# Gated recurrence and gated state-space block on one core: the opening in chunks, weights loaded later, two turns in another order

## The chip, the cores and the metric

The kernel runs on one core of one Trainium2 chip. The metric is the time of one execution on the device in microseconds (us). A core has a matrix engine (PE, TensorE) with its own weight load (PEld), a vector engine (DVE), a scalar engine (ACT), a GpSimd engine (POOL) and a sync engine (SP) that here only issues transfers (DMAs). Each engine works through its own list of instructions in order; semaphores tie the lists together. SBUF is the on-chip memory of 128 partitions, PSUM the eight banks into which PE writes.

## The reference, cut to what matters

A gated linear recurrence over 4 batches, 8 heads, 768 steps and a head width of 48, whose output, heads side by side, is the input of a gated state-space block:

```
for t in range(768):                       # q, k, v, alpha: (4, 8, 768, 48)
    state = alpha[t][:, None] * state + outer(k[t], v[t])
    y[t] = q[t] @ state
x = heads side by side                     # (4, 768, 384)
val, gate = split(x @ w_in)                # w_in (384, 1024)
h[t] = exp(A_log[0]) * h[t-1] + val[t]     # a scan, per channel
out = (silu(gate) * h) @ w_out             # w_out (512, 384)
```

All inputs are float32 but w_in and w_out, which arrive as 64-bit floats and are made into float32 on the chip.

## The kernel before, in words

The 4 x 768 steps are cut into 12 groups of 256 steps. Group m goes through the recurrence as follows (lines of the kernel before).

- Its alpha, q and k are loaded (L410 for whole tiles, L421 for the first groups) with steps on partitions and are turned so that the head width lies on partitions: for groups 0 to 3 by PE against an identity (`turned`, L680, either by matmuls, L694, or by transposes, L689 and L690) with copies out of PSUM by ACT (L702) or DVE (L701); from group 4 on by DVE itself (`turn`, L595).
- Two scans on DVE give the running products P of alpha from the front (`scan_P`, L630) and V from the back (`scan_V`, L649). k times V gives Zk (L614), q times P gives Zq (L605).
- `scores` (PE, L744) multiplies Zk with Zq in blocks of 64 steps, `masks` cuts them to the lower triangle: on DVE (L754, L759), ACT (L756, L760, L764) and, from group 3 on, POOL (L762).
- `values` (PE, L778; for group 0 L862) gives the part of y from the own block, `states` (PE, L810) each block's contribution to the state, which POOL (`add_up`, L828, L830) or DVE (`add_banks`, L838; group 0: L879) adds up; `carried` (PE, L791; group 0: L870) applies the states to q.
- `join` copies y out of PSUM (ACT, L904, L905) and moves the pieces of heads to their places in xT by DMA (L907), issued by SP and POOL; group 0 needs no moves (`first_join`, L884).

Then the second block: `project(n, cc)` (PE, L927) multiplies group n's xT by one of four 128-column units of w_in, val first, then gate, into two PSUM banks; DVE scans val (L932), ACT takes silu of the gate (L940), DVE or POOL multiplies them (L942). `output(n)` (PE, L956) multiplies by w_out, ACT copies the result (L950), SP stores it.

The weights' 64-bit words are loaded in units (`load_w`, L453; `load_w_out`, L459) and converted in three parts: `low` on ACT (L544), two operations on DVE (L553, L555), an integer add on POOL (L557). Before, unit 2 of the loads holds the third and fourth 128 columns together.

The order is written by hand: what the Python code calls first stands first in every engine's list. The loop over n (turn n) projects group n while group n + 1 or n + 2 goes through the recurrence. In a steady turn: `second(n+1)` (values, states, sums), four projections with steps of DVE's work for a later group between them (`go(count)` runs that many of the seven steps of `products`: turn a, scan P, turn k, scan V, Zk, turn q, Zq), `third(n+1)` (carried, values, join), `first(n+2)` (scores, masks), and `output(n)`. Four PSUM banks named mm are shared in rotation by turns, projections, outputs and the second half of the scores.

Of the kernel before, what the change touches and what calls it, by code (L numbers as in the profile page):

```python
# [346 lines left out]
def fast(  # L347
# [22 lines left out]
    nc = tc.nc  # L370
# [18 lines left out]
    p2 = pool("p2", 2)  # L389
    ps_at = pool("ps_at", 1, space=PS)  # L390
# [56 lines left out]
    units = [range(0, 1), range(1, 2), range(2, 4)]  # L447
# [45 lines left out]
    def constants():  # L493
# [45 lines left out]
    def low(i):  # L539
        bits, w = bits_of(i)  # L540
        r = p2.tile([C, UW], I32, tag="wr", name="wr")
        lows[i] = r.rearrange("p (a n) -> p a n", a=w.shape[1])
        halves = lows[i].bitcast(U16).rearrange("p a (n two) -> p a n two", two=2)
        nc.scalar.activation(halves[:, :, :, 0], bits[:, :, :, 0], AF.Copy, scale=2.0 ** -29)  # L544

    def convert(i):
        if i not in lows:
            low(i)
        bits, w = bits_of(i)
        r = lows.pop(i)  # L550
        halves = r.bitcast(U16).rearrange("p a (n two) -> p a n two", two=2)
        quarters = bits.rearrange("p a n two -> p a (n two)").bitcast(U16).rearrange("p a (n four) -> p a n four", four=4)
        nc.vector.tensor_scalar(out=w.bitcast(U32), in0=bits[:, :, :, 1], scalar1=3, scalar2=0x3FFFFFFF,  # L553
                                op0=ALU.logical_shift_left, op1=ALU.bitwise_and)
        nc.vector.tensor_scalar(out=halves[:, :, :, 1], in0=quarters[:, :, :, 3], scalar1=0xC000, scalar2=None,  # L555
                                op0=ALU.bitwise_and)
        nc.gpsimd.tensor_tensor(out=w.bitcast(I32), in0=w.bitcast(I32), in1=r, op=ALU.add)  # L557
# [126 lines left out]
    def turned(m, name, js, t):  # L684
        raw = steps_of(name, m)
        tp = t[:, 0:len(js) * C].rearrange("p (j x) -> p j x", j=len(js))
        if (m, name) in ((1, "k"), (1, "q"), (3, "a")):
            for n, j in enumerate(js):
                nc.tensor.transpose(tp[:, n], raw[:, ds(ROW + j * D - 64, C)], ident)  # L689
                nc.tensor.transpose(tp[0:64, n], raw[:, ds(j * D, 64)], ident)  # L690
            return tp.rearrange("p j (c h) -> p h c j", h=4)
        for n, j in enumerate(js):
            for i in range(2):
                nc.tensor.matmul(tp[ds(64 * i, 64), n], raw[:, ds(i * ROW + j * D, 64)], ident,  # L694
                                 start=True, stop=True, skip_group_check=True)
        return tp.rearrange("p j (c h) -> p h c j", h=4)

    def copy_turned(to, js, tp, engine=None):
        place = by_runs(to)[:, :, :, js.start:js.stop]
        if engine:  # L700
            return engine.tensor_copy(out=place, in_=tp)  # L701
        return nc.scalar.activation(place, tp, AF.Copy)  # L702

    def turn_over(m, name, to, tags=(None, None)):
        size = NJ // len(tags)
        copies = []
        for n, tag in enumerate(tags):
            js = range(size * n, size * (n + 1))
            copy = copy_turned(to, js, turned(m, name, js, bank(tag)), nc.vector if n % 2 and tag else None)
            if tag:  # L710
                for other in copies[(n + 1) % 2::2]:
# [3 lines left out]
    def alphas(m, tags=(None, None)):  # L715
        turn_over(m, "a", by_place(als[m % 2])[:, :, 1:GP], tags)
# [31 lines left out]
    def masks(m):  # L748
        sc = [[t[:, 0:4 * (L + D)].rearrange("p (h x) -> p h x", h=4) for t in pair] for pair in scs.pop(m)]
        mb = mask[:, None, :]  # L750
        if m < NG:
            for c in range(G):
# [162 lines left out]
    def project(n, cc, late=False):  # L915
# [10 lines left out]
        for vg, kk in order:  # L926
            nc.tensor.matmul((pv, pg)[vg], w_ins[cc][:, kk, vg, :], xT[:, kk, :],  # L927
                             start=(kk == 0), stop=(kk == NK - 1))
# [10 lines left out]
        sg = p2.tile([C, GC], FP32, tag="sg", name="sg")  # L939
# [43 lines left out]
    alphas(0, ("s0", "s1", "y1", "y0"))  # L983
    tq = straighten(0, "q")
    tk = straighten(0, "k")
    alphas(1)
    P = scan_P(0)
    V = scan_V(0, P, False)
    halves = [range(0, NJ // 2), range(NJ // 2, NJ)]
    parts = [turned(1, "k", js, bank()) for js in halves]  # L990
# [3 lines left out]
    scores(0)  # L994
    tk = plain("k")
    for js, part in zip(halves, parts):
        copy_turned(tk, js, part)
    low(0)
    parts = [turned(1, "q", js, bank()) for js in halves]
    convert(0)  # L1000
    nc.gpsimd.memset(raws["a"][0:1, 0:1], 0.0)
    load_steps("a", 2, [nc.sync])
    load_w(units[2], nc.sync)
    masks(0)
    low(1)
    first_values(True)
    st = states(0)
    convert(1)
    first_states(st)
    tq = plain("q")  # L1010
    for js, part in zip(halves, parts):
        copy_turned(tq, js, part)
    last = P[:, :, GC]
    nc.scalar.activation(ratio[:, 0], last, AF.Copy, scale=1.0 / FIRST_PRODUCT)
    nc.scalar.activation(lower[:, :, 0], last, AF.Copy)
    for name in "kqa":
        load_steps(name, 2 + (name == "a"), [nc.sync])
    load_v(1, nc.sync)
# [31 lines left out]

    for n in range(N):
        m = n + 1
        if n == 0:
            V = scan_V(1, P)
            f0 = project(n, 0)
# [3 lines left out]
            f1 = project(n, 1)  # L1059
            convert(2)  # L1060
            alphas(2)
            low(3)
            first(m)
            f0()
            f1()
            tk = straighten(2, "k")
            load_raw("k", 3, nc.sync)
            P = scan_P(2)
            tq = straighten(2, "q")
            V = scan_V(2, P)  # L1070
            convert(3)
            junk(1)
            low(4)
            f2 = project(n, 2)
            values(m, True)
            st = states(m)
            add_banks(m, st)
# [8 lines left out]
        elif n == 1:  # L1086
# [8 lines left out]
            add_banks(m, st)  # L1095
            f3()
# [26 lines left out]
        else:  # L1123
            if n == 2:
                first(m)
                go(1)
                f0 = project(n, 0)
                second(m)
                go(2)
            else:  # L1130
                second(m)
                go(4)
                f0 = project(n, 0)
            f0()
# [11 lines left out]
            load_raw("q", n + 3, nc.sync)  # L1146
# [4 lines left out]
            go(1)  # L1151
# [3 lines left out]
            first(m + 1)  # L1155
# [8 lines left out]
        if 0 < n < N - 1:  # L1164
            output(n)
    return value
# [61 lines left out]
```

## Time and profile before

| | us |
|---|---|
| timed runs, median (lowest to highest of 3) | 279.6 (279.18 to 279.66) |
| profiled execution | 279.43 |
| its span | 277.7 |
| PE busy | 268.8 |
| DVE busy | 218.3 |
| POOL busy | 122.4 |
| ACT busy | 108.6 |

The span runs from the first to the last instruction; the profiled execution's own time is 1.73 us longer. In a row of the timeline or of the chain of waits stand the start and the length in us, the engine, the line and what was written; in brackets is the idle time of the engine before it and what ended it. Matmuls in float32 appear in the trace as two rows each, transposes as one. PE's granted clock is 1.00 over the whole span.

### The profile page before, as it was taken

The page shows a single profiled execution, that of the slowest core. Times are in us where ns is not written, and L with a number is a line of the kernel's source. Part 1 is how long each engine was busy: PE and PEld are TensorE (multiplying, and loading weights), DVE is VectorE, ACT ScalarE, POOL GpSimd, SP SyncE. Part 2 cuts the span into 40 slices and gives each one's busy share as a digit, 9 for nine tenths or more (in the row PEclk, how much of TensorE's full clock was granted, in tenths as well). Part 3 has the DMA queues.
Part 4 walks back from the last instruction along what each step waited for, and adds up shares of the span by engine and source line. Part 5 has one row for each costly group of instructions (what it writes and reads, how often), then busy time and mean ns, then how long its engine had stood idle before and what let it go on. Part 6 is the DMA issues. An engine that isn't in the chain of part 4 may idle for free.

```text
span 277.7 us, 9598 instructions
## 1 busy us (share of the span) xinstructions
PE 268.8 (97%) x4056; PEld 217.0 (78%) x4056; DVE 218.3 (79%) x281; ACT 108.6 (39%) x244; POOL 122.4 (44%) x141
## 2 busy tenths in 40 slices
PE   7999999999989999899999999999999999999995
PEld 5988887876678688488688688688688688787874
DVE  7979998898798995995895995996995993079540
ACT  2577763461332532341542433433434425213111
POOL 8141223130068574563473584484384476435000
PEclk9999999999999999999999999999999999999999
DMA  6949993845919777487468587576687501201201
GB/s 196 295 140 309 296 262 78 205 88 139 267 48 238 149 199 182 103 214 163 103 181 199 114 205 164 130 197 155 152 186 159 144 0 27 77 1 33 71 5 59
DMA packets 51599, 41.18 MB, mean 148 GB/s; under 512 B 27360, under 2 KB 49536, under 8 KB 51552
## 3 DMA queue, kind: packets, MB, share of 16 engines
q1 hardware_dynamic: 48752, 37.50, 53.1%
q0 software_dynamic: 1408, 2.03, 2.8%
q10 hardware_dynamic: 1392, 0.99, 1.2%
q8 instruction: 33, 0.54, 0.9%
q14 instruction: 14, 0.11, 0.2%
HBM read 32.54 MB, written 4.72 MB: 134 GB/s over the span
## 4 chain that ended last, share of the span: by engine, by line
PE 92%; DVE 3%; DMA 1%; POOL 1%; issue 1%; ACT 1%; SPq 0%; DVEq 0%; ACTq 0%
PE mm L927 45%; PE mm L956 21%; PE y L791 4%; PE y L778 4%; PE mm L744 3%; PE s L744 3%; PE s L810 3%; PE mm L694 2%; PE mm L1189 2%; DMA raw_a<-in_alpha_dram 1%; POOL AK L762 1%; DVE P L630 1%; DVE V L649 1%; PE mm L689 1%; PE y L862 1%
## 5 line engine op out<-in xcount | busy, mean ns | idle before, releaser
L927 PE MATMUL mm<-xT,w_in 128*128 128x256 f32 x576 | 128.9, 382 | 0.6 <-ACT xT L884 0.6
L927 PEld LDWEIGHTS mm<-xT,w_in 128*128 128x128 f32 x576 | 108.1, 190 | 16.3 <-issue 0.8
L956 PE MATMUL mm<-w_out,f_last 128*128 128x384 f32 x160 | 54.1, 492 | 1.3 <-DVE A L759 1.3
L940 ACT ACTIVATE sg<-mm 128x256 f32<-128x256 f32 x48 | 18.4, 384 | 85.8 <-PE mm L927 80.3
L956 PEld LDWEIGHTS mm<-w_out,f_last 128*128 128x128 f32 x160 | 29.7, 190 | 21.1 <-issue 1.4
L830 POOL TENSOR_TENSOR sum<-sum,dS 128x192 f32<-128x192 f32 x30 | 33.2, 1108 | 27.3 <-PE mm L927 13.5
L942 POOL TENSOR_TENSOR f_last<-sg,hh 128x256 f32<-128x256 f32 x36 | 30.9, 862 | 30.6 <-ACT sg L940 23.1
L932 DVE TENSOR_TENSOR_SCAN hh<-a_dec,hh,mm 128x256 f32<-128x256 f32 x32 | 23.4, 732 | 15.4 <-PE mm L927 15.2
L630 DVE TENSOR_TENSOR_SCAN P<-al,lower 128x1028 f32<-128x1028 f32 x12 | 31.1, 2595 | 0.6
L649 DVE TENSOR_TENSOR_SCAN V<-al,ends 128x1028 f32<-128x1028 f32 x12 | 28.3, 2356 | 0.4
L907 POOL DMA_DIRECT2D xT<-yst x40 | 20.5, 517 | 13.1 <-ACT yst L904 11.8
L950 ACT ACTIVATE o_sb<-mm 128x384 f32<-128x384 f32 x22 | 10.8, 491 | 38.4 <-PE mm L956 38.4
L762 POOL TENSOR_TENSOR AK<-AK,mask 128x512 f32<-128x512 f32 x9 | 13.2, 1464 | 17.2 <-ACT AK L760 17.2
L759 DVE TENSOR_TENSOR A<-s,mask 128x256 f32<-128x256 f32 x9 | 3.8, 425 | 21.5 <-PE s L744 21.5
L557 POOL TENSOR_TENSOR w_in<-w_in,wr 128x768 int32<-128x768 int32 x4 | 7.3, 1826 | 26.0 <-DVE wr L555 17.0
L595 DVE STREAM_TRANSPOSE k<-raw_k 128x1024 f32<-128x1024 f32 x9 | 18.3, 2033 | 0.0
L595 DVE STREAM_TRANSPOSE q<-raw_q 128x1024 f32<-128x1024 f32 x9 | 18.2, 2022 | 0.0
L778 PEld LDWEIGHTS y<-AK,v 64*64 64x64 f32 x352 | 12.1, 134 | 6.4 <-issue 5.0
L595 DVE STREAM_TRANSPOSE al<-raw_a 128x1024 f32<-128x1024 f32 x8 | 16.3, 2041 | 0.1
L778 PE MATMUL y<-AK,v 64*64 64x64 f32 x352 | 14.5, 221 | 1.0 <-POOL AK L762 1.0
L791 PEld LDWEIGHTS y<-Zq,sum 48*64 48x64 f32 x656 | 11.8, 134 | 4.3 <-issue 4.1
L791 PE MATMUL y<-Zq,sum 48*64 48x64 f32 x656 | 14.4, 221 | 0.6 <-issue 0.6
(158 smaller groups left out, 392.2 us busy)
## 6 DMA issues: line engine op xcount, KB each, us to landing
v<-in_v_dram SPq DMA_DIRECT2D x22, 192.0 KB, 3.3
out_dram<-o_sb SPq DMA_DIRECT2D x22, 192.0 KB, 2.1
raw_k<-in_k_dram SPq DMA_DIRECT2D x18, 184.0 KB, 3.4
raw_q<-in_q_dram SPq DMA_DIRECT2D x18, 184.0 KB, 3.8
raw_k<-in_k_dram SPq DMA_DIRECT2D x18, 176.0 KB, 3.8
raw_q<-in_q_dram SPq DMA_DIRECT2D x18, 176.0 KB, 4.1
raw_a<-in_alpha_dram SPq DMA_DIRECT2D x16, 184.0 KB, 5.0
raw_a<-in_alpha_dram SPq DMA_DIRECT2D x16, 176.0 KB, 5.1
```

The source lines that it names most:

```text
L595: nc.vector.transpose(out=by_runs(to).rearrange("p h c j -> p h j c"), in_=raws[name][:, 0:4 * ROW].rearrange("p (h j d) -> p h j d", h=4, ...
L630: nc.vector.tensor_tensor_scan(out=P, data0=al[:, 0:4 * GP], data1=lower.rearrange("p h t -> p (h t)"), initial=0.0, op0=ALU.mult, op1=ALU ...
L649: nc.vector.tensor_tensor_scan(out=V[:, ::-1], data0=al[:, 1:4 * GP + 1][:, ::-1], data1=ends.rearrange("p h t -> p (h t)")[:, ::-1], init ...
L778: nc.tensor.matmul(ys[m][i][ds(64 * s, 64), e, ds(c * C + h * L, L)], v_sb[rows, c, 4 * i + p, :], As[i][rows, c, p, :], start=across and ...
L791: nc.tensor.matmul(ys[m][i][ds(64 * s, 64), e, ds(u * L, L)], Ss[j][rows, p, :], Zqs[m % 2][rows, u, p, D:], start=False, stop=True, skip_ ...
L830: nc.gpsimd.tensor_add(Ss[j][:, :, 0:D], Ss[j - 1][:, :, 0:D], part)
L907: engines[n % len(engines)].dma_start(out=xT[to, a], in_=st[rows, i, e])
L927: nc.tensor.matmul((pv, pg)[vg], w_ins[cc][:, kk, vg, :], xT[:, kk, :], start=(kk == 0), stop=(kk == NK - 1))
L932: nc.vector.tensor_tensor_scan(out=hh, data0=a_dec[:, cc:cc + 1].to_broadcast([C, GC]), data1=pv, initial=prev_h[cc][:, GC - 1:GC] if n % ...
L940: nc.scalar.activation(sg, pg, AF.Silu)
L942: f = lambda: engine.tensor_mul(fs[n][cc], sg, hh)
L956: nc.tensor.matmul(os[c], fs[n][cc][:, ds(c * C, C)], w_outs[cc // 2][:, cc % 2, :], start=(cc == 0), stop=(cc == NI - 1))
```

## The change

It has five parts.

1. **Opening by chunks.** The first group's alphas are turned by 32 matmuls of 64 x 64 (`first_alphas`) instead of 16 of 128 x 64, and those that need only the half of the heads whose DMA is issued on ACT's queue come first. The first q is turned in an order by halves (`first_q`). The first k and the second alpha are turned by transposes. Memsets on DVE go: those of the sums' pad columns become copies on ACT, those of dS and K0 fall away. Of the second k only one half is turned ahead of the first scores, the other behind them; the first half of the **second q** is turned behind the states, the other, by matmuls, behind the carried work. The masks of group 0 stand ahead of the first weights' conversion on DVE.
2. **Second weights behind the scans.** The conversion of w_in's second unit is split: `low(1)` behind `first_join`, `high(1)` behind the scans P and V of group 1, `add_low(1)` behind the first projection. The alphas of group 2 are turned between the first and the second projection. Units 2 and 3 are loaded apart, unit 3 behind k, q and alpha. The signal that lets alpha of group 2 be loaded over the old one is an ACT copy from the last state's sum instead of a POOL memset.
3. **Projection in halves.** In turn 0 the gate half of `project(0, 2)` stands behind values and states of group 1 (`between`). The products of silu and scan for the first two projections move from turn 0 to turn 1, and the silu tiles have a pool of four buffers.
4. **w_out** is loaded behind the moves of y of group 1 and no longer in the opening; k, q and alpha of group 3 are loaded behind it.
5. **Two turns reordered** (`late = (1, 3)`). In turn 2 and turn 4 `second(n+1)` stands behind the second projection instead of ahead of or behind the first. In turn 3 `first(5)` stands behind `output(3)` instead of ahead of it. In turn 4 the steps of `go` and the loads are spread anew.

```diff
-    units = [range(0, 1), range(1, 2), range(2, 4)]
+    units = [range(i, i + 1) for i in range(NI)]
...
-        for t in dS[0] + dS[1]:
-            nc.vector.memset(t[:, :, :, D:64], 0.0)
-        for t in sums:
-            nc.vector.memset(t[:, :, D:64], 0.0)
-        nc.vector.memset(K0[:, :, :, D:], 0.0)
...
+    def first_alphas():
+        raw, to = steps_of("a", 0), by_runs(by_place(als[0])[:, :, 1:GP])
...
+        def turn_quarter(j, i, r):
+            rows = ds(64 * r, 64)
+            nc.tensor.matmul(tps[j // 4][r][ds(64 * i, 64), j % 4], raw[rows, ds(i * ROW + j * D, 64)],
+                             ident[rows, rows], start=True, stop=True, skip_group_check=True)
+
+        for j in range(2):
+            for r in range(2):
+                turn_quarter(j, 1, r)
+        for j in range(NJ):
+            for r in range(2):
+                turn_quarter(j, 0, r)
+                if j + 2 < NJ:
+                    turn_quarter(j + 2, 1, 1 - r)
...
+                copy = nc.vector.tensor_copy(out=place, in_=part) if r else \
+                    nc.scalar.activation(place, part, AF.Copy)
...
-    def project(n, cc, late=False):
+    def project(n, cc, late=False, between=None):
...
+        passes(order[:NK] if between else order)
...
+        if between:
+            between()
+            passes(order[NK:])
+        sg = gates.tile([C, GC], FP32, tag="sg", name="sg")
...
-    alphas(0, ("s0", "s1", "y1", "y0"))
-    tq = straighten(0, "q")
+    first_alphas()
+    for t in sums:
+        nc.scalar.activation(t[:, :, D:64], wide_S[0][:, 0:4 * (64 - D)].rearrange("p (j d) -> p j d", j=4), AF.Copy)
+    tq = first_q()
     tk = straighten(0, "k")
     alphas(1)
     P = scan_P(0)
...
     V = scan_V(0, P, False)
...
+    part = turned(1, "k", halves[0], bank())
     for c in range(G):
         scaled_k(0, tk, V, c)
         scaled_q(0, tq, P, c)
...
+    for c in range(G):
+        scores(0, (c,))
+    part = turned(1, "k", halves[1], bank())
+    masks(0)
+    low(0)
+    high(0)
+    add_low(0)
+    copy_turned(tk, halves[1], part)
+    first_values(True)
+    st = states(0)
+    part = turned(1, "q", halves[0], bank())
+    first_states(st)
+    copy_turned(tq, halves[0], part)
+    nc.scalar.activation(raws["a"][0:1, 0:1], sums[3][0:1, 0, 0:1], AF.Copy)
     load_steps("a", 2, [nc.sync])
     load_w(units[2], nc.sync)
...
+    load_w(units[3], nc.sync)
     load_v(1, nc.sync)
     P = scan_P(1)
     first_carried((1,))
     first_values(False)
     first_carried((2, 3))
+    part = turned(1, "q", halves[1], bank(), False)
     first_join()
+    low(1)
+    copy_turned(tq, halves[1], part)
...
-    for half in range(2):
-        load_w_out(half, nc.sync)
...
         if n == 0:
             V = scan_V(1, P)
-            f0 = project(n, 0)
+            high(1)
+            fs_late = [project(n, 0)]
+            add_low(1)
+            alphas(2)
...
-            f1 = project(n, 1)
+            fs_late.append(project(n, 1))
             convert(2)
-            alphas(2)
...
+            f2 = project(n, 2, between=across_and_states)
             alphas(3)
             third(m)
-            for name in "qa":
+            for half in range(2):
+                load_w_out(half, nc.sync)
+            for name in "kqa":
                 load_raw(name, 3 + (name == "a"), nc.sync)
...
+    late = (1, 3)
...
             if n == 2:
                 first(m)
-                go(1)
-                f0 = project(n, 0)
-                second(m)
-                go(2)
-            else:
+            if n - 1 not in late:
                 second(m)
                 go(4)
-                f0 = project(n, 0)
+            else:
+                go(n // 2)
+            f0 = project(n, 0)
             f0()
-            load_raw("k", n + 3, nc.sync)
-            load_raw("a", n + 3, nc.sync)
-            go(1)
+            if n == 2:
+                go(2)
+            if n != 4:
+                load_raw("k", n + 3, nc.sync)
+                load_raw("a", n + 3, nc.sync)
+                go(1)
             f1 = project(n, 1)
             f1()
+            if n - 1 in late:
+                second(m)
+            if n == 4:
+                go(2)
+                load_raw("k", n + 3, nc.sync)
+                load_raw("a", n + 3, nc.sync)
...
-            go(1)
+            go(2 if n == 4 else 1)
+            load_raw("q", n + 3, nc.sync)
             f3 = project(n, 3)
             f3()
             third(m)
-            first(m + 1)
+            if n not in late:
+                first(m + 1)
...
         if 0 < n < N - 1:
             output(n)
+        if n > 1 and n in late:
+            first(m + 1)
```

More of the change, by code (lines that the diff above doesn't have):

```diff
@@ L548, in convert @@
             low(i)
[L549 to L557, printed above, removed]
+        high(i)
+        add_low(i)
     def check_w(i):
@@ L696, in turned @@
         return tp.rearrange("p j (c h) -> p h c j", h=4)
[L698 to L705, printed above, removed]
-        copies = []
[L707 to L711, printed above, removed]
+    halves = [range(0, NJ // 2), range(NJ // 2, NJ)]
@@ L718, in straighten, with turn_over, alphas @@
+    def turn_over(m, name, to):
+        for js in halves:
+            copy_turned(to, js, turned(m, name, js, bank()))
+    def alphas(m):
+        turn_over(m, "a", by_place(als[m % 2])[:, :, 1:GP])
     def straighten(m, name):
@@ L987, in fast @@
     P = scan_P(0)
+    last = P[:, :, GC]
+    nc.scalar.activation(ratio[:, 0], last, AF.Copy, scale=1.0 / FIRST_PRODUCT)
+    nc.scalar.activation(lower[:, :, 0], last, AF.Copy)
     V = scan_V(0, P, False)
-    halves = [range(0, NJ // 2), range(NJ // 2, NJ)]
-    parts = [turned(1, "k", js, bank()) for js in halves]
+    part = turned(1, "k", halves[0], bank())
     for c in range(G):
@@ L993, in fast @@
         scaled_q(0, tq, P, c)
[L994 to L997, printed above, removed]
[L998 to L1001 removed]
+    tk, tq = plain("k"), plain("q")
+    copy_turned(tk, halves[0], part)
+    for c in range(G):
+        scores(0, (c,))
+    part = turned(1, "k", halves[1], bank())
+    masks(0)
+    low(0)
+    high(0)
[7 more added lines that the diff above has]
+    nc.scalar.activation(raws["a"][0:1, 0:1], sums[3][0:1, 0, 0:1], AF.Copy)
     load_steps("a", 2, [nc.sync])
     load_w(units[2], nc.sync)
[L1004 to L1015, printed above, removed]
     for name in "kqa":
         load_steps(name, 2 + (name == "a"), [nc.sync])
+    load_w(units[3], nc.sync)
     load_v(1, nc.sync)
```

85 lines of the change are left out of this document (59 added, 26 removed).

## The prediction, made before the changed kernel was run

> **What bounds the kernel now.** I read the page's busy line and chain first, then what PE waited for.
>
> ```profile
> span 277.7 us, 9598 instructions
> PE 268.8 (97%) x4056; PEld 217.0 (78%) x4056; DVE 218.3 (79%) x281; ACT 108.6 (39%) x244; POOL 122.4 (44%) x141
> ...
> PE 92%; DVE 3%; DMA 1%; POOL 1%; issue 1%; ACT 1%; SPq 0%; DVEq 0%; ACTq 0%
> ```
>
> PE (the matrix engine) is busy for 97% of the span and carries 92% of the chain that ends last. The profiled execution took 279.43 us, 1.73 beside its span of 277.7; the three timed runs have a median of 279.6. The change takes next to no work off PE, so it can only gain where PE stands idle, and it loses wherever it makes PE wait anew. The waits of PE, by releaser (total, times, longest):
>
> ```profile
> PE mm L956 <- DVE A L759: 1.3, 1, 1.3
> PE y L778 <- POOL AK L762: 1.0, 1, 1.0
> PE y L791 <- issue: 0.6, 1, 0.6
> PE mm L927 <- ACT xT L884: 0.6, 1, 0.6
> ```
>
> These four are 3.5 us, plus the opening, where PE works behind two DVE scans. That is what there is to win.
>
> **Part 1, the opening.** The chain of waits (start, length, what), then the timeline of the helpers:
>
> ```profile
> 4.79 1.56 PE s L694 x16
> 6.35 0.91 PE y L694 x16
> ...
> 7.87 2.31 DVE P L630
> ...
> 15.47 1.00 PE mm L744 x32
> ...
> 20.28 0.62 PE y L870 x22
> ...
> 23.39 5.42 PE mm L927 x24
> 28.81 1.90 PE mm L694 x32
> 30.71 0.93 PE s L744 x32
> ```
>
> ```profile
> 7.29 0.47 DVE L701 COPY al<-y 128x256 f32<-128x256 f32 x1 [0.43 <-PE y L694]
> ...
> 15.24 0.55 DVE L553 TENSOR_SCALAR w_in<-wbits 128x768 uint32<-128x768 uint32 x1
> 15.71 0.62 DVE L555 TENSOR_SCALAR wr<-wbits 128x768 uint16<-128x768 uint16 x1
> ...
> 21.67 2.30 DVE L630 TENSOR_TENSOR_SCAN P<-al,lower 128x1028 f32<-128x1028 f32 x1
> ...
> 24.42 2.30 DVE L649 TENSOR_TENSOR_SCAN V<-al,ends 128x1028 f32<-128x1028 f32 x1
> ```
>
> ```profile
> 19.93 1.82 POOL L557 TENSOR_TENSOR w_in<-w_in,wr 128x768 int32<-128x768 int32 x1 [0.64 <-DVE wr L555]
> ```
>
> The new `first_alphas` turns the first alphas by 32 matmuls of 64x64 (64 rows of the trace) instead of 16 of 128 rows. The 64x64 form is priced by L778:
>
> ```profile
> 42.47 0.47 PE y L778 x32
> 43.50 0.65 issue
> ```
>
> 32 rows in 0.47 is 0.94 us for 64. The first 16 old rows took 1.56 and the next 16 0.91, so PE is slower just there; I take 1.4 us, an estimate between 0.94 and twice that, from 4.79 to 6.2, where the old form ended at 7.26. Two copies on each of ACT and DVE (0.47 each) follow: 5.95 to 6.9. DVE's memsets that went to ACT or went away stand ahead of the first copy and are hidden now. The first scan P so starts at about 6.95 instead of 7.87: a gain of 0.9. Bounds: nothing (if the second half of alpha lands late), and 1.3 (all 64 rows at the full rate). With it the scores' second half starts at 14.55 (was 15.47).
>
> From there PE's order differs. Before, 16.47 to 20.28 (3.81) held all of the second q's turn (1.90) and values and states (1.91). After, it is half a k turn (0.95), values and states (1.91), half a q turn (0.95), then the 2.55 us of carried work (20.28 to 23.39 less the 0.56 wait), then the other half of q (0.95), which now covers the wait on xT. Sum: 15.55 + 0.95 + 1.91 + 0.95 + 2.55 + 0.95 = 22.9, against 23.39.
>
> But the second weights, converted before the scan in the old order, are now behind it. DVE's second P started 1.39 after the states' end (20.28 to 21.67); the states now end at 18.4, so P is at 19.8 and V ends at 24.85. Then `high(1)` on DVE (15.24 to 16.21, when the next starts: 0.97) and the add on POOL (1.82): the second weights are ready at 27.75. PE does the first projection (2.7, half of 5.42) to 25.6 and the alphas of group 2 (1.90) to 27.5, waits 0.25, and does the second projection to 30.5. The next scores are at 30.5 against 30.71: **-0.2**. Most of what the chunks gain is handed to the weights behind the scans. Bounds: -0.6, if the chunks give 1.3; +0.6, if they give nothing.
>
> **Part 2, the idle time at 43.50.** It stands in a run of short matmuls and no semaphore in the trace ends it. The same "issue" is part of the stall at 112. What lies between the two, and the page's queue of instructions:
>
> ```profile
> 43.60:112.10 68.50, 66.33 (x1015) 52.82 (x1014) 58.40 (x67) 26.30 (x61) 30.01 (x30) 1.00 0.67 158
> ```
>
> ```profile
> q8 instruction: 33, 0.54, 0.9%
> ```
>
> 1015 matmuls and 1014 weight loads, with a score of waits, are eight times 256; 33 packets of 16.4 KB for PE's 8112 rows are about 246 each. I read both as PE running out of fetched instructions after a block of some 256 short ones. The change puts half of a projection (1.4 us) into that block, between the states and the turn of alpha, so the block lasts 1.4 us longer, more than the 0.65 that was waited: **-0.65**, or nothing if it is something else.
>
> The Trainium skill, "Runtime: NRT & Kernel Launch", section "Instruction fetch mechanics", states blocks of 256 instructions fetched while the block before runs, and that crossing a block's end is mostly hidden. The block's size agrees with the distance above; if it is hidden here too, the 0.65 is another wait and stays, and the sum below would be 279.4.
>
> **Part 3, turn 2.** `second(3)` moves behind the second projection, so PE no longer waits 1.0 for POOL's mask.
>
> ```profile
> 75.88 3.03 POOL L762 TENSOR_TENSOR AK<-AK,mask 128x512 f32<-128x512 f32 x1 [17.21 <-ACT AK L760]
> ```
>
> ```profile
> 75.56:88.56 13.00, 12.91 (x14) 1.00 0.57 142
> ```
>
> ```profile
> 89.67 0.77 PE s L744 x32
> ```
>
> With 5.3 us of projections ahead of it the mask (3.03) is hidden. What is late next is DVE: from the scan at 75.56 to the end of Zq at 88.56 it works without a gap (12.91 of 13.00), and the next scores need that Zq. They come at 88.65 instead of 89.67: **-1.0**. POOL's three sums now stand behind f1; if they run late the gain shrinks to -0.4.
>
> **Part 4, turn 4.** `first(5)` moves behind `output(3)`, which removes the 1.3 at L956. The chain, DVE's rows, and DVE's window:
>
> ```profile
> 110.02 0.77 PE s L744 x32
> ...
> 112.81 5.40 PE mm L956 x16
> 118.21 0.62 PE y L778 x32
> ...
> 131.65 0.77 PE s L744 x32
> ```
>
> ```profile
> 111.61 0.42 DVE L759 TENSOR_TENSOR A<-mm,mask 128x256 f32<-128x256 f32 x1 [0.34 <-PE mm L744]
> ...
> 114.29 2.74 DVE L630 TENSOR_TENSOR_SCAN P<-al,lower 128x1028 f32<-128x1028 f32 x1
> ```
>
> ```profile
> 112.18:128.18 16.00, 15.75 (x14) 1.00 0.70 170
> ```
>
> Here the same move costs. In DVE's order all work for group 6 (the turn of alpha, P, k, V, Zk, q, Zq, and three scans of projections) stands behind the two masks A of group 5. Before, it had from 112.18 to the scores at 131.65, 19.5 us, for 16.0 us of work, because the 5.40 us of output stood inside. Now output(3) runs 110.02 to 115.42, the scores 115.42 to 117.03, and the second mask A starts at 117.01 (1.59 after the scores, as 111.61 to 110.02). DVE's chain follows 0.34 to 0.57 later (the idle time in the row of A; 111.61 to 112.18) and takes 15.3 us (15.75 busy, with P at 2.30 instead of 2.74) to 16.0: Zq is done at 132.65 to 133.6. PE, which needs 13.44 (118.21 to 131.65) from the end of the scores, is there at 130.5 and waits. The scores of group 6 come 1.0 to 1.95 later than 131.65. I take **+1.2**: POOL's mask will no longer lie beside P, its sums still beside V. Later turns have their output inside again and keep their 20 us.
>
> The 2.74 belongs to a P beside POOL's mask. The Trainium skill, "SBUF — State Buffer", states that a DVE operation with two SBUF inputs and a GpSimd operation that reads SBUF lock each other out for a whole instruction. The mask of 3.03, beside the scan that opens the window of turn 2, agrees; the sum by it is that of the slow rival below.
>
> **Part 5, w_out.** It is issued behind the moves of y.
>
> ```profile
> 28.98 3.21 SPq L459 DMA_DIRECT2D wobits<-in_moe_w_out_dram  x2
> ...
> 45.19 3.15 SPq L907 DMA_DIRECT2D xT<-yst  x4
> ```
>
> ```profile
> wobits<-in_moe_w_out_dram SPq DMA_DIRECT2D x2, 768.0 KB, 7.4
> ```
>
> ```profile
> 55.08 1.07 ACT L544 ACTIVATE wr<-wobits 128x768 uint16<-128x768 uint32 x1
> ```
>
> ```profile
> 60.56 5.16 PE mm L956 x16
> ```
>
> On a clock 0.85 earlier by then, the moves are issued by 47.5, the second half of w_out 1.6 later, and at the 7.4 of the old, crowded place it lands by 56.5; ACT's 1.07 and POOL's 1.82 make it 59.4. Output(0) starts at 59.7 and takes up that half after four of its 16 rows, 1.3 us on: hidden, with 1.6 us to spare. Queued behind it on SP are k, q, a and v of group 3; DVE takes k up only behind the two conversions of w_out itself, so these loads are needed later, too. Cost 0, upper bound +1.5.
>
> **What is costed at nothing.** The pad columns of the sums, now written by ACT between its copies of alpha and q, hide behind PE's turn of q. The two gate products of the opening move behind the sums of turn 1; their cover is the rest of turn 1, before the next scores need DVE, and without it they cost their own length. The loads of group 3 in the order k, q, a only change places behind one another on SP, and the gates' four buffers take a wait away that no row shows.
>
> **Sum.** -0.2 - 0.65 - 1.0 + 1.2 = -0.65: 279.43 - 0.65 = **278.8 us**.
>
> **The rivals.**
> *The fast one: turn 4 is not DVE-bound.* If DVE's chain hides, the scores of group 6 come at 130.5, -1.2 instead of +1.2: 276.4. For it: DVE has nothing to do while output(3) runs and could have worked ahead. Against it: in the order of its instructions nothing of group 6 stands ahead of the masks of group 5. Chance 0.2.
> *It does not do what it says:* the issue stall only moves and the opening's gain goes wholly into the second weights: 0 + 0 - 1.0 + 1.2 gives 279.6. Chance 0.15.
> *The slow one: DVE and POOL block each other in both turns.* POOL's sums, now beside DVE's q and Zk work in turn 2, hold third(3) until the old time (0 instead of -1.0), and in turn 4 they stretch the scans to the 16.0 chain (+1.95). -0.2 - 0.65 + 1.95 is +1.1: 280.5. It decides from the point where POOL's last sum of group 3 ends a microsecond behind the start of third(3), and where V of group 6 has to wait for POOL. Chance 0.15.
> *w_out late,* from a landing after 58.1 on, one for one; with its bound of 1.5, 280.3. Chance 0.05.
>
> **How the numbers follow.** The forecast has 0.45, with its own range from 278.0 to 279.6. The range reaches into both outer cases, 276.6 to 280.4. About 0.2% (0.56 us) is what a measurement of this kernel can tell from no change. Faster by more: 0.33 of the forecast and the fast rival, 0.53; within: 0.12 of the forecast and most of the third case, 0.25; slower: 0.22.
>
> **What would show it.** P of group 0 at 7.0; the second projection waiting for POOL's add; no idle time near 43; scores of group 4 right behind Zq; above all a wait of 2 us or more of L790's scores on DVE's Zq in turn 4. Without that wait I am wrong by the fast rival; with a wait of PE on POOL's sums in turn 2, or of output(0) on w_out, by a slow one.

## The result and the profile after

The changed kernel takes 288.07 us (median of 6, 286.95 to 289.07), the kernel before 279.55 (median of 6): a ratio of 1.0305, interval 1.0277 to 1.0333. I had predicted 278.8 and a range up to 280.4, so size, sign and range were all wrong. The profiled execution took 288.29 with a span of 286.6.

The page of the changed kernel, span, busy times, granted clock in 40 slices, and the shares of the chain:

```profile
span 286.6 us, 9641 instructions
...
PE 274.6 (96%) x4060; PEld 220.5 (77%) x4060; DVE 218.9 (76%) x270; ACT 109.2 (38%) x251; POOL 114.9 (40%) x140
...
PEclk9999999999979999999599999999999999999999
...
PE 84%; DVE 8%; issue 2%; DMA 2%; ACT 1%; POOL 1%; SPq 0%; DVEq 0%; ACTq 0%; POOLq 0%
```

Two things are new. Of the chain PE has 84% where it had 92%, DVE 8% instead of 3%, transfers (DMA) 2% instead of 1%. And PE is busy for 5.8 us more with almost the same matmuls: in two slices the clock is below full, which it never was before. What PE waited for in the changed kernel (total, times, longest):

```profile
PE mm L974 <- ACT o_sb L1002: 4.2, 1, 4.2
PE s L790 <- DVE Zq L609: 2.8, 1, 2.8
...
```

The chain of waits of the changed kernel (start, length, what), cut to the marks, then three rows of the chain of the kernel before that the prediction did not show:

```profile
27.85 2.86 PE mm L974 x12
30.71 0.93 PE s L790 x32
...
43.68 0.77 PE s L790 x32
...
67.47 3.88 PE mm L1008 x12
...
72.61 5.31 DMA out_dram<-o_sb
...
78.57 7.13 PE mm L974 x24
...
93.75 0.77 PE s L790 x32
...
114.10 5.36 PE mm L1008 x16
119.45 0.93 PE s L790 x32
...
137.58 1.77 PE s L790 x32
139.35 1.49 PE mm L790 x32
140.85 6.70 PE mm L1008 x16
147.55 0.62 PE y L824 x32
```

```profile
44.54 0.76 PE s L744 x30
...
68.31 5.16 PE mm L956 x16
...
138.55 0.62 PE y L778 x32
```

Mark against mark, this is where the 8.9 us of the spans went:

| stretch | before | after | difference |
|---|---|---|---|
| start to the scores of group 1 | 30.71 | 30.71 | 0 |
| to output(1) | 37.60 (to 68.31) | 36.76 (to 67.47) | -0.84 |
| to the scores of group 4 | 21.36 (to 89.67) | 26.28 (to 93.75) | +4.92 |
| to the end of third(4) | 20.35 (to 110.02) | 20.35 (to 114.10) | 0 |
| to the end of output(4) | 28.53 (to 138.55) | 33.45 (to 147.55) | +4.92 |
| to the end | 139.15 | 139.05 | -0.1 |

The first +4.92 is the wait of 4.2 on a row buffer for the output, and a pair of projections that took 7.13 where the same 24 rows take 5.38 elsewhere (+1.75), less the 1.0 of the mask that is no longer waited for. The second is a delay of 3.0 (at the old pace PE is through its 13.44 us of work after the scores' end at 121.15 by 134.6; it was through at 134.8, stood idle for 2.8, and the scores of group 6 start at 137.58), scores of 3.26 instead of 1.54, an output of 6.70 instead of 5.36, and 0.16 of slower scores at 119.45, less the 1.25 of idle time between the scores and the output of before. The windows of the changed kernel say why the same work takes longer (columns: PE, PEld, DVE, ACT, POOL busy, granted clock, share of the DMA engines, GB/s):

```profile
78.00:80.00 2.00, 1.43 (x4) 1.16 (x5) 0.00 (x0) 1.91 (x5) 0.00 (x0) 0.67 0.60 168
80.00:82.00 2.00, 2.00 (x6) 1.60 (x5) 0.54 (x1) 0.39 (x2) 1.26 (x1) 0.50 0.29 104
82.00:84.00 2.00, 2.00 (x10) 1.72 (x9) 2.00 (x3) 0.85 (x2) 0.39 (x1) 0.98 0.00 0
...
136.00:140.00 4.00, 2.42 (x52) 2.45 (x56) 2.48 (x4) 1.11 (x3) 1.70 (x3) 0.59 0.89 203
140.00:144.00 4.00, 4.00 (x26) 2.38 (x19) 3.08 (x3) 1.03 (x4) 2.34 (x4) 0.56 0.66 148
```

At the end of the first long wait, and within the second, the clock falls to half, stays there for some microseconds while PE is at work again, and is then full. A window's mean tells how long: 0.67 of 2 us is 1.3 at half, so it fell at 78.7, and 0.98 in the third window puts the end at 82.1; in turn 4, 0.59 and 0.56 of 4 us are 3.3 and 3.5 at half, from 136.7 to 143.5.

The first wait begins on SP. SP's issues in the kernel before, then in the changed one (start, time from the first to the end of the last of a group, what):

```profile
60.94 1.75 SPq L410 DMA_DIRECT2D raw_k<-in_k_dram  x4
...
69.42 1.20 SPq L951 DMA_DIRECT2D out_dram<-o_sb  x2
```

```profile
46.93 1.09 SPq L460 DMA_DIRECT2D wobits<-in_moe_w_out_dram  x2
48.13 2.11 SPq L411 DMA_DIRECT2D raw_k<-in_k_dram  x4
50.34 4.60 SPq L411 DMA_DIRECT2D raw_q<-in_q_dram  x4
55.92 2.77 SPq L411 DMA_DIRECT2D raw_a<-in_alpha_dram  x4
...
61.17 4.69 SPq L411 DMA_DIRECT2D raw_k<-in_k_dram  x4
65.96 4.96 SPq L953 DMA_DIRECT2D xT<-yst  x8
...
72.61 0.99 SPq L1003 DMA_DIRECT2D out_dram<-o_sb  x2
```

Two of SP's waits in the changed kernel between 44 and 80 us, then the first k part of group 4 alone:

```profile
SPq L411 <- DVE lower L644: 3.3, 1, 3.3
SPq L411 <- DMA wobits<-in_moe_w_out_dram: 3.0, 2, 2.5
```

```profile
61.17 3.25 SPq L411 DMA_DIRECT2D raw_k<-in_k_dram  x1
```

Four q parts of group 3 take 4.60 and four k parts of group 4 take 4.69, where the kernel before needs 1.96 and 1.75. The two have different causes. In front of the third and the fourth q part SP stands until w_out's two transfers have landed, the second at 54.6; in SP's order each is the eighth transfer before the part that waits for it, and in the trace SP's transfers use eight semaphores in turn, each only when the transfer that used it before has landed. So alpha goes out at 55.92 instead of 50.49, and v after it. Of the k parts it is the first one's issue that lasts 3.25 us, and it does not wait for w_out, which has landed. The row names DVE's L644, but DVE had read the old k by 61.15 (its turn of k starts at 59.10 and takes 2.05), and in the kernel before the same issue takes 0.33. What differs is the crowd: at its start seven earlier transfers of SP had not landed, before none. In all six profiles of kernels with both loads moved on SP seven are under way there, and the issue takes 3.25 to 3.94; with four or five it takes 1.1 to 1.4, with three or none 0.33. By which means the crowd holds an issue, the trace does not say.

So the stores of output(0), last in this line, go out at 72.61 instead of 69.42, though PE is 0.84 earlier, and they land at 77.9, after 5.31 where the first of them took 3.13 before. `output` has two row buffers; output(1) needs them back from 72.1 on. ACT cannot evict, PE gets no free PSUM bank for the next projection, and stands still.

### The profile page after: what moved, and what is told of

It reads as the page before. It is cut to its first block, busy times and chain, and to the rows that moved or that the text cites. A ratio compares the mean times of both kernels' runs of the same rounds, so it can differ in the third digit from the quotient of the medians.

```text
span 286.6 us, 9641 instructions
## 1 busy us (share of the span) xinstructions
PE 274.6 (96%) x4060; PEld 220.5 (77%) x4060; DVE 218.9 (76%) x270; ACT 109.2 (38%) x251; POOL 114.9 (40%) x140
## 4 chain that ended last, share of the span: by engine, by line
PE 84%; DVE 8%; issue 2%; DMA 2%; ACT 1%; POOL 1%; SPq 0%; DVEq 0%; ACTq 0%; POOLq 0%
PE mm L974 42%; PE mm L1008 20%; PE y L837 4%; PE y L824 4%; PE mm L790 3%; PE s L790 3%; PE s L856 3%; DMA out_dram<-o_sb 2%; PE mm L1257 2%; DVE V L653 2%; DVE P L634 2%; PE mm L700 1%; PE y L772 1%; DVE Zk L618 1%; DVE hh L981 1%
## 5 line engine op out<-in xcount | busy, mean ns | idle before, releaser
L974 PE MATMUL mm<-xT,w_in 128*128 128x256 f32 x576 | 131.4, 386 | 4.4 <-ACT o_sb L1002 4.2
L1008 PE MATMUL mm<-w_out,f_last 128*128 128x384 f32 x160 | 55.5, 501 | 0.0
L1008 PEld LDWEIGHTS mm<-w_out,f_last 128*128 128x128 f32 x160 | 30.3, 194 | 20.6 <-issue 1.5
L876 POOL TENSOR_TENSOR sum<-sum,dS 128x192 f32<-128x192 f32 x30 | 31.4, 1045 | 22.1 <-ACT dS L864 12.4
L808 POOL TENSOR_TENSOR AK<-AK,mask 128x512 f32<-128x512 f32 x9 | 11.4, 1265 | 25.8 <-ACT AK L806 25.8
L618 DVE TENSOR_TENSOR Zk<-k,V 128x1024 f32<-128x1024 f32 (+1 forms) x14 | 16.4, 1173 | 0.1
L790 PE MATMUL s<-Zq,Zk 48*64 48x112 f32 x384 | 12.4, 270 | 2.8 <-DVE Zq L609 2.8
L609 DVE TENSOR_TENSOR Zq<-q,P 128x1024 f32<-128x1024 f32 (+1 forms) x14 | 14.8, 1055 | 0.1
```

What stands on the lines that cost most here:

```text
L618: nc.vector.tensor_mul(Zks[m][:, ds(c0, n)].rearrange("p c h t -> p h c t"), t[:, :, at].rearrange("p h (c t) -> p h c t", t=C), V[:, :, 1 ...
L790: nc.tensor.matmul(scs[m][c][i][ds(L * h, L), ds(p * (L + D), L + D)], Zk[rows, c, p, ds(h * L, L)], Zq[rows, u, p], start=True, stop=True ...
L876: nc.gpsimd.tensor_add(Ss[j][:, :, 0:D], Ss[j - 1][:, :, 0:D], part)
L1008: nc.tensor.matmul(os[c], fs[n][cc][:, ds(c * C, C)], w_outs[cc // 2][:, cc % 2, :], start=(cc == 0), stop=(cc == NI - 1))
```

## The experiments

Times are medians, beside the 278.9 to 279.4 of the kernel before on the same chip.

**w_out back in the opening.**

```diff
+    for half in range(2):
+        load_w_out(half, nc.sync)
     load_v(2, nc.sync)
...
             third(m)
-            for half in range(2):
-                load_w_out(half, nc.sync)
```

> The changed kernel with the two loads of w_out back in the opening, where the kernel before had them; all else as changed. Theory (SP's queue): the two loads of 768 KB and what stands behind them make SP issue the stores of output(0) at 72.6 instead of 69.4, the row buffers of output(1) come free only at 77.9, PE waits 4.2 us and then runs 1.75 us slower at a granted clock of 0.50. Without the loads at that place both go: 288.07 - 4.24 - 1.75 = 282.1 us, PE's wait on o_sb is gone, second(3) starts near 79.7. Rival (the load of k of group 3, which moved to the same place, holds SP): PE's wait on o_sb stays above 2 us, and the time above 285. Second rival (first(4) and the masks reordered in turn 2): wait stays at 4.2, 288.

282.39 us (ratio 1.0102, 1.0077 to 1.0126). What PE still waited for, longest row:

```profile
PE s L790 <- DVE Zq L609: 2.8, 1, 2.8
```

The row of o_sb is gone, the stores go out at 68.35: the theory's 282.1 holds, both rivals fall. That SP's first k part is held here too, but only for 1.10 us, fits a loss that needs both w_out and k there.

**Four row buffers.**

```diff
-    NBUF = 3
+    NBUF = 2
...
-    rows = ctx.enter_context(tc.tile_pool(name="rows", bufs=2))
+    rows = ctx.enter_context(tc.tile_pool(name="rows", bufs=4))
```

> The changed kernel with four row buffers for the output instead of two (and, to make room, two instead of three pad buffers in the fallback that does not run). SP's order and all loads stay as changed, so the stores of output(0) are as late as before this edit. Theory (the late store only matters through the row buffer): the wait of 4.24 and the slow 1.75 go, 282.1 us, although SP issues that store near 72.6. Rival (the transfers themselves are what PE suffers from, by late loads or a busy memory): another wait appears in the same place, and the time stays above 286.

283.42 us. SP is as late as in the changed kernel, and PE does not wait for it:

```profile
73.61 0.99 SPq L1003 DMA_DIRECT2D out_dram<-o_sb  x2
```

From output(1) to the scores of group 4 this run needs 20.37 (67.66 to 88.03), as the run with w_out in the opening does (67.14 to 87.51). So in this stretch the late store costs through the two buffers and in no other way; the 1.0 by which the time lies above 282.39 arises outside it.

**Only k of group 3 back.**

```diff
             tk = straighten(2, "k")
+            load_raw("k", 3, nc.sync)
...
-            for name in "kqa":
+            for name in "qa":
```

> The changed kernel with only the load of k of group 3 back behind the turn of k of group 2; w_out stays behind the moves of y. Theory (SP's queue is held: in the changed kernel the third part of q of group 3 waits for the landing of the first w_out, the eighth transfer before it): with four transfers fewer SP does not come to a wait on w_out before the v of group 3, the stores of output(0) go out near 69.5, PE's wait on o_sb falls below 1 us, 282 to 283.3 us. Rival (the bytes of w_out, 1.5 MB at that time, are what delays everything): the wait stays above 3 us, 287.

282.87 us; four of the five runs lie from 281.4 to 283.0. The fifth, the profiled one, took 286.26: it has an idle time in the opening, which other kernels with this opening show, too (last section). In its profile there is no wait on o_sb, SP still waits 2.2 for w_out, and the first k part takes 0.33.

**w_out issued by POOL.**

```diff
-                load_w_out(half, nc.sync)
+                load_w_out(half, nc.gpsimd)
```

> The changed kernel with the two loads of w_out issued by POOL instead of SP, at the same place behind the moves; the same bytes at about the same time, k of group 3 still behind them on SP. Theory (SP's queue is held by the slow landing of w_out): SP no longer waits for it, the stores of output(0) go out by 70.5, the wait on o_sb falls below 2 us and the clock stays near 1.00: 282 to 284 us. Rival (bytes): SP's stores still near 72.6, wait 4 us, 288.

284.74 us: neither theory in full. PE's waits, then SP's:

```profile
PE mm L974 <- DVE hh L981: 1.5, 1, 1.5
...
PE mm L974 <- ACT o_sb L1002: 0.2, 1, 0.2
```

```profile
SPq L411 <- DMA raw_k<-in_k_dram: 6.6, 4, 4.4
```

The wait on o_sb is all but gone, but w_out and k now crowd each other: DVE waits 5.26 for w_out's second half, to 59.0, and PE waits for DVE (1.5, and 1.3 in output(0)). SP waits for parts of k instead, again the eighth transfers before. The stores go out at 73.82 even so; PE, late itself, hardly waits for them. Moving w_out off SP's queue does not move its bytes out of the way.

**Turn 4 as before**, first with the order on PE alone:

```diff
-    late = (1, 3)
+    late = (1,)
```

> The changed kernel with turn 4 as it was (first(5) ahead of output(3)); turn 2, the opening and w_out stay as changed. Theory: from the end of third(4) to the end of output(4) the changed kernel took 33.45 us (114.10 to 147.55) and the kernel before 28.5 (110.02 to 138.55); undone it is 28.5 again: 288.07 - 4.9 = 283.2 us, with a wait of about 1.3 before output(3) back. Rival (the slow stretch at 134 to 148 is an echo of the stall at 74): the time stays above 286.5.

291.77 us, slower still. The edit left the turn's counts of `go` as changed, which belong to the other order, so it says nothing of the theory; what it shows is that DVE running two steps ahead brings PE new waits:

```profile
PE mm L1008 <- ACT AK L806: 4.3, 3, 1.4
...
PE y L824 <- POOL AK L808: 2.3, 2, 2.1
```

Then with the steps of `go` and the loads of that turn as before, too:

> The changed kernel with turn 4 wholly as it was, DVE's steps and SP's loads of that turn too (the run before this one put back only the order on PE, so that DVE ran two steps ahead of its place from turn 4 on and PE met new waits, 4.3 us on ACT's AK, 2.3 on POOL's AK, 1.4 on POOL's f_last). Theory: 288.07 - 4.9 = 283.2 us, the wait on Zq gone, about 1.3 before output(3) back, clock 1.00 after 90. Rival (the slow stretch at 134 to 148 is an echo of the stall at 74): above 286.5.

283.81 us; the wait on Zq is 0.2, and the only long one is that on o_sb (4.9 here). An idle time of 0.8 without a releaser stands inside the scores of group 5. Either loss goes while the other stays.

**PE kept busy in the wait for Zq.**

```diff
+                if n == 4:
+                    t = bank("s0")
+                    for _ in range(12):
+                        nc.tensor.matmul(t[:, 0:256], wide_S[0][:, 0:C], wide_S[0][:, 0:256], start=True,
+                                         stop=True, skip_group_check=True)
                 first(m + 1)
```

> The changed kernel with 12 matmuls of 128x256 on idle data put on PE between the last projection of turn 4 and the scores of group 6, some 2.6 us of work in a wait of 2.9; their result is not read. Theory (the idle time lowers the granted clock): the scores still start near 137.6, since DVE's Zq sets that, but the clock stays at 1.00 from 136 to 144, the scores take 1.54 instead of 3.26 and output(4) 5.36 instead of 6.70: 288.07 - 3.06 = 285.0 us. Rival (scores and output are slow because transfers or DVE and POOL crowd them): they stay slow, 288 us or, with the added matmuls, more.

289.33 us, because the added work outlasted the wait. With 6 instead of 12:

> The changed kernel with 6 instead of 12 added matmuls of 128x256 on idle data ahead of the scores of group 6: each turned out as two passes of 0.22, so 12 filled 5.39 us, 2.4 more than the wait, while the clock stayed at 1.00 and output(4) took 5.36. With 6 they fill 2.7 of the wait of 2.9. Theory (idle time lowers the clock): 288.07 - 3.06 = 285.0 us. Rival (the clock follows the wait's end, not PE's idle time): clock below 0.7 between 136 and 144, 288.

286.13 us. Its chain and its windows:

```profile
138.49 1.00 PE s L790 x32
...
140.25 5.36 PE mm L1008 x16
```

```profile
136.00:138.00 2.00, 2.00 (x11) 1.77 (x10) 1.97 (x2) 1.45 (x4) 0.00 (x0) 1.00 0.74 155
138.00:140.00 2.00, 1.94 (x66) 1.54 (x65) 1.37 (x3) 0.36 (x1) 0.84 (x2) 1.00 0.97 247
```

Same wait for Zq, but idle matmuls in it: the clock stays at 1.00, the scores and the output are back at 1.77 and 5.36, and the stretch from third(4)'s end (114.95) to output(4)'s end (145.61) is 30.66 instead of 33.45. The 2.8 gained is the price of the low clock. The total fell by less, 1.9, because the other stall of this run was longer in its profile (8.05 for the slow projections instead of 7.13).

**Both undone**, w_out in the opening and turn 4 as before:

> Both losses undone: w_out loaded in the opening and turn 4 wholly as before; the opening by chunks, the split projection, the late gate products and the reordered turn 2 stay. Theory: the two losses add, 282.39 - 4.9 = 277.5 us, 1.9 below the kernel before, of which the issue idle (-0.65 to -0.86) and turn 2 (-1.0) are the parts. Rival (turn 2's gain is given back where DVE's and POOL's work of the turns after comes late): 278.5 to 279.5.

278.95 us (278.04 to 281.09), ratio 1.0000 (0.9973 to 1.0028): the losses are gone, the forecast gain shows only in part. In its profile the scores of group 4 stand at 88.10, 1.57 ahead of before, and part of that is given back to an idle time of 1.4 without a releaser inside the next scores. So the reordered turn 2 is no gain in the time of this kernel: the run without it, below, takes 278.37.

**DVE's steps for group 6 ahead of the masks of group 5**, w_out in the opening; two steps, then three (`go(3)`, and one fewer behind the third projection):

```diff
-                go(n // 2)
+                go(n // 2 if n == 2 else 0)
...
+        if n == 3:
+            go(2)
         if 0 < n < N - 1:
             output(n)
```

> w_out in the opening, turn 4 as changed (first(5) behind output(3)), but DVE's first two steps for group 6, the turn of alpha and the scan P (2.05 + 2.30 us), are put ahead of the masks of group 5, into the 5 us in which DVE was idle while output(3) ran. Theory (DVE's chain behind the masks sets the wait): Zq comes 4.3 us earlier, PE does not wait, the clock stays at 1.00: 282.39 - 2.97 - 3.06 = 276.4 us. Rival (the chain is set by POOL's sums or by the loads): the wait stays above 1 us and the time above 279.

278.24 us (0.9947 to 1.0006). The scores of group 6 wait only 1.27, named after ACT, though Zq ended last, at 131.21, and the clock is 1.00 there:

```profile
131.36 1.00 PE L790 MATMUL s<-Zq,Zk 48*64 48x112 f32 x32 [1.27 <-ACT yst L951]
```

> As the run with alpha's turn and P of group 6 ahead of the masks of group 5, with DVE's turn of k (2.0 us) put ahead as well. In that run the scores of group 6 still waited 1.2 us, Zq ending at 131.2 while PE was there at 130.2, with the clock at 1.00; DVE stood idle for 3.5 us before the masks. Theory (DVE's chain): Zq comes about 2 us earlier, the wait goes: 278.24 - 1.2 = 277.0 us. Rival (an idle time of about 1.3 us without a releaser, as at 110 in the run with turn 4 as before, falls into this turn): 278.2.

276.72 us (276.56 to 276.93), ratio 0.9913 (0.9897 to 0.9930): 0.9% below the kernel before, and the lowest of all runs. PE's only named wait of the whole span stands at the very start, and its chain has the scores of group 4 20.37 us behind output(1), where the kernel before needs 21.36:

```profile
PE y L772 <- DVE raw_q L499: 1.4, 1, 1.4
```

```profile
67.27 5.16 PE mm L1008 x16
...
87.64 1.00 PE s L790 x32
```

**The opening alone** (w_out in the opening, turns 2 and 4 as before):

> The new opening, the split projection, the late gate products and the new order of group 3's loads alone: w_out is loaded in the opening, and turns 2 and 4 are wholly as before. Theory by the marks of the runs so far (scores of group 1 at 30.7 in both, scores of group 2 at 43.7 to 44.0 instead of 44.5): 0.5 to 0.85 below the kernel before, 278.5 us, if the opening shows no idle time of its own; in three of seven profiles it has 0.3 to 0.9 without a releaser. Rival: that idle time is in most executions, 279.2, no difference.

278.37 us, ratio 0.9980 (0.9964 to 0.9997): a small gain, as expected. With turn 2 as before, PE's wait of 1.0 on POOL's mask is back.

Two questions were left, and both were put on the fastest kernel. **The third projection in one piece:**

```diff
-            f2 = project(n, 2, between=across_and_states)
+            f2 = project(n, 2)
+            across_and_states()
```

> The fastest kernel so far (three DVE steps ahead, w_out in the opening, 276.72 us, no wait of PE after 7 us) with the third projection of group 0 in one piece ahead of the values and states of group 1, as in the kernel before. Theory of the prediction (a run of some 256 short matmuls without a projection in it outlasts the fetch of the next instructions): the idle time without a releaser is back near 42.5, 0.5 to 0.9 us, and the time is 277.4. Rival (the idle time hangs on where the program's blocks fall, or on other traffic): no idle time there, 276.7.

277.14 us (276.54 to 280.98), and in the chain of the profiled execution, which took 278.17:

```profile
43.30 1.41 issue
```

The idle time is back at its old place, and longer. But six of the twelve executions lie between 276.5 and 277.0, and ten of the eleven executions of the two kernels with the split projection lie between 276.3 and 277.2. Either the idle time is not in all executions or it costs little in them; that the split shortens the time is not shown.

**w_out behind the moves, k of group 3 early:**

> The fastest kernel so far with w_out behind the moves of y, as in the changed kernel, but with k of group 3 loaded where the kernel before had it. Theory (either load alone fits into the time before the stores of output(0), only both together hold SP's queue): no wait on o_sb, 276.7 us. Rival (w_out's place costs by itself): a wait on o_sb or on DVE of over 0.5 us between 60 and 80, above 277.3.

276.79 us, no wait on o_sb. SP's rows:

```profile
61.21 1.77 SPq L411 DMA_DIRECT2D raw_k<-in_k_dram  x4
...
69.71 1.09 SPq L1003 DMA_DIRECT2D out_dram<-o_sb  x2
```

SP waits 3.4 for w_out here, longer than in the changed kernel, but in front of alpha's parts, and the stores go out in time all the same: the wait for w_out is not what makes them late. At the first k part three transfers are under way, and it takes 0.33. So w_out's new place costs nothing by itself, and neither does k's (276.72). Only both together hold SP.

## Why the prediction was wrong, step by step

- **Opening, -0.2:** nearly right. P of group 0 came at 7.12 (I said 6.95), the second projection waited for POOL's add as said (27.85 against 27.75, where my own terms 24.85, 0.97 and 1.82 add up to 27.64); a projection of 12 rows measured 2.79 to 2.86, not half of 5.42, and the scores of group 1 came at 30.71, as before: 0.
- **Idle time at 43.50, -0.65:** right in the profiles, open in the time. The scores of group 2 stand 12.97 behind those of group 1 (43.68 less 30.71) instead of 13.83, -0.86; no profile of a kernel with the split projection has the idle time, and that of the unsplit one has it again. But half of the unsplit kernel's executions are as fast as the others. That it is instruction fetch remains a reading. The Trainium skill, "Runtime: NRT & Kernel Launch", section "Instruction fetch mechanics", calls a block's end mostly hidden; if this is one, 0.65 and 1.41 us of it are not hidden in these two profiles.
- **Turn 2, -1.0:** right in the turn itself. 21.36 became 20.37 where nothing else stood in it. With turn 4 as before the time did not show it (278.95 with it, 278.37 without).
- **w_out, cost 0:** this step failed, at the sentence "Queued behind it on SP are k, q, a and v of group 3; DVE takes k up only behind the two conversions of w_out itself, so these loads are needed later, too." Its landing was right: DVE's second conversion started at 54.63, and output(0) did not wait. But I stopped the queue at group 3. Behind it on the same queue stand k of group 4, the moves of group 2 and the stores of output(0), and the two row buffers hang on these. With k's loads behind w_out the alphas go out 5.4 later, seven transfers are under way when k of group 4 is due, its first issue lasts 3.25, and the stores go out 3.2 late and land 2.2 slower. A wait of 4.24 us and 1.75 of low clock followed: +6.0, where my bound was +1.5.
- **Turn 4, +1.2:** the mechanism was right, the size not. Zq set the scores, and the idle time of 2.8 lies in the 2.15 to 3.1 that my two chains give (132.65 to 133.6 less 130.5); V took 2.74 beside POOL's sums, as bounded. The term that failed is the price of a wait: I counted its length. The halved clock behind it added 3.06 (1.72 in the scores, 1.34 in the output), so +4.92 in place of +1.2. The 1.25 that I took off as a wait on DVE's mask is for the larger part an idle time without a releaser: the mask A ends at 112.03 and the output starts at 112.81, and when turn 4 is put back 0.8 to 1.4 stand as "issue" inside the scores of group 5.
- **Rivals:** the one of w_out late had the right edit and the wrong wait. The slow one saw the sign but neither the store nor the clock.

The Trainium skill, "TensorE: Matmul & The Clock Gate", section "HAM oscillation — how this bites in real kernels", warns of idle gaps of PE above some 3.4 us. I did not weigh it: no wait that I forecast was that long. The runs here are stricter: gaps of 1.27, 1.5 and 2.1 left the clock at 1.00, gaps of 2.7, 2.8 and 4.2 halved it.

## What to carry to other kernels

A load that is moved must be followed down its queue to the last thing that waits there, stores too, and from a store to the buffers that come free with its landing; count what is then under way at once, since each of two moves alone can be free and both together not. A wait of PE costs its length while it is short, and here about one and a half to two times that once it was long enough to halve the clock (4.2 cost 6.0, 2.8 cost 5.9). Work that stands behind a handover in an engine's order without needing it (DVE's steps for group 6 behind the masks of group 5) can be taken ahead of it, into the time in which the engine stands idle: that turned the loss of turn 4 into a small gain.

## What the runs showed of the hardware

- In turn 4 the clock fell to 0.50 1.9 us into the wait (at 136.7, with PE idle from 134.8) and stayed there for 6.8 us. At the wait on o_sb it fell 4.3 us behind the wait's start (at 78.7, with PE idle from 74.3) and stayed for 3.4. The four changes stand 3.4, 54.6 and 6.8 us apart, which is 1, 16 and 2 times 3.41; in the run with only k early they are 1, 33 and 2 times 3.41 apart. So the clock seems to change only in steps of some 3.41 us, and the same wait can cost one step or two: with w_out on POOL the wait of 2.8 for Zq got 3.4 us at half (135.6 to 139.0) instead of 6.8, and of the four other executions with only k early two took 281.4 and 281.5 at a mean clock of 0.994 (3.4 us at half), two 282.9 and 283.0 at 0.988 (6.7 us). Where the steps fall was not controlled.
- The new opening has an idle time without a releaser in 6 of 15 profiles, mostly 0.3 to 0.9 us, once 2.67. Its row, and the window behind it, of the run with only k early:

```profile
16.61 2.67 issue
```

```profile
20.00:22.00 2.00, 2.00 (x89) 2.00 (x85) 0.03 (x1) 0.33 (x1) 0.00 (x0) 0.50 0.03 8
```

  It halved the clock, too, and the scores of group 1 came at 34.29. It probably makes the wide spread of these kernels (276.5 to 281.0 in the unsplit run): the three executions there from 279.9 on have a mean clock of 0.993 or 0.994, which is 3.3 to 3.9 us at half. What decides whether it comes was not tried and stays open.
